# The second tile's q taken by the casting queue, the start of an attention-plus-feed-forward kernel put in a new order, and the first tile's denominators by halves

## Chip, cores, metric

One core of one Trainium2 chip. The metric is the time of one execution on the device in microseconds (us), inputs and outputs in device memory. The runs of one kernel in one block lie within 0.3 us (after_again) to 3.7 us (q_early) of each other, so small differences are judged over several runs on the same chip. On one core a run counts as fast unless it is over 1.5% above the fastest of its kernel; all runs told here are within that (the two single looks have no state of their own).

## The reference, cut to what matters

```python
# attention without softmax: 8 batches, 8 heads, 576 positions, head size 64
r_q, r_k = maximum(q, 0), maximum(k, 0)
q_p = concat(r_q * cos_w, r_q * sin_w)      # cos_w, sin_w depend on the position
k_p = concat(r_k * cos_w, r_k * sin_w)
kv  = einsum('bhsf,bhsd->bhfd', k_p, v)
den = einsum('bhsf,bhf->bhs', q_p, sum(k_p, axis=2)) + 1e-6
x   = einsum('bhsf,bhfd->bhsd', q_p, kv) / den
# feed-forward: x is [4608, 512], inner size 1536
g   = x @ w_gate
out = (g * sigmoid(g) * (x @ w_val)) @ w_out
```

All of it is float32 outside; the kernel multiplies in bf16.

## The kernel before, the parts that matter

The 576 positions of a batch lie in nine slots of 64. A tile is two slots, 128 rows of x. For the first four tiles the order of work at the start is a hand-laid list of words that a loop turns into instructions.

```python
CUT = (4, 7)
first = {"q": consts.tile([P, G, CUT[0], D], FP32, name="first_q")}
...
def load_first(nm, gs, lo=0, hi=NC):          # SyncE's queue, float32
    nc.sync.dma_start(out=first[nm][:, gs, lo:hi]..., in_=source(0, nm)[:, gs, lo * D:hi * D])
KCUT = 5
load_first("v", slice(0, 2))
load_first("v", slice(2, 4))
load_first("q", slice(0, G), 0, 2)            # slots 0, 1: tile 0
load_first("k", slice(0, 2))
load_first("k", slice(2, 4), 0, KCUT)
load_first("k", slice(2, 4), KCUT, NC)
load_first("q", slice(0, G), 2, 4)            # slots 2, 3: tile 1, last in this queue
...
def load_slots(b, nm, lo, hi):                # GpSimd's queue: casts to bf16 on the way
    nc.gpsimd.dma_start(out=raw_of(b, nm)[:, :, lo:hi]..., in_=source(b, nm)[:, :, lo * D:hi * D])
...
nc.gpsimd.tensor_copy(out=hold, in_=first["v"][:, 1, 0, 0:1])   # GpSimd waits for the first half of v
load_slots(0, "q", CUT[0], NW)                # slots 4 to 7
load_w(0, 1); load_w(1, 1); ...               # then the weights, k and v of batch 1, and so on
...
words = """
    cq0@act cq1@act tq0 qr0@dve rk1.0@act rk0.0@dve qw0.0 qw0.1 z6 kv0.0 rk2.0@act rk3.0@dve rk2.1@act
    kv1.0 kvo01@dve rk3.1@act cq3@dve kv1.1 cq2@dve kvo00@dve tq1 kvo10@act a0.0 qr1@dve kvo11@act qw1.1
    z2 a0.1 qw1.0 tq2 den0 rec0 a1.0 x0.0 qr2@act tq3 x0.1 xt0.0 a1.1 qw2.0 xc0.0@act xt0.1 qw2.1
    ... """
```

The words: cq casts q of one slot to bf16; tq transposes a tile's q on TensorE; qr is its relu; qw weights it with cos and sin; rk is the relu of a piece of k; kv the products k times v; kvo copies them out of PSUM; a are the products of a tile's q with kv; den, rec, x make x from them; xt and xc turn x; G, s, V, m are the feed-forward part; z are idle products on zeros that keep TensorE busy. After the @ stands the engine (act is ScalarE, dve VectorE).

## Time and profile before

| | before |
|---|---|
| time, median of 3 runs | 327.97 us (327.35 to 328.61) |
| span of the profiled run | 326.1 us |
| TensorE busy | 318.7 us, 98% |
| TensorE idle, waiting for q of tile 1 | 1.71 us |

TensorE is busy nearly all the time, so busy shares say little. What can be won is read from the list of its waits and from its timeline before 20 us. Both are in the prediction.

### The profile page before, as it was taken

What the parts mean: (1) busy time and instruction counts of PE and PEld (TensorE: products, weight loads), DVE (VectorE), ACT (ScalarE), POOL (GpSimd) and SP (SyncE); (2) the same over time, 40 slices, a digit from 0 to 9 for tenths busy, and PEclk for the clock granted to TensorE, in tenths of its full rate; (3) what the DMA queues carried; (4) which work ended last, traced back from release to release, by engine and by line L of the source; (5) the groups of instructions that cost most, each with busy time, mean ns of one, the idle gap of its engine ahead of it and who ended that gap; (6) DMA issues with size and microseconds to landing.
All of it is one profiled execution on the core that took longest, in us unless ns stands there. A gap on an engine that the chain in (4) does not pass through costs nothing.

```text
span 326.1 us, 6192 instructions
## 1 busy us (share of the span) xinstructions
PE 318.7 (98%) x2459; PEld 165.0 (51%) x2470; DVE 182.3 (56%) x367; ACT 132.8 (41%) x248; POOL 34.1 (10%) x57
## 2 busy tenths in 40 slices
PE   8799999999999999999999999999999999999995
PEld 4488855454545444544454445444454445444443
DVE  7594857885575655575557555655664145423420
ACT  7353456843463336423543344343432133213311
POOL 6654300002001100020002000200000000000000
PEclk9999999999999999999999999999999999999999
DMA  7999999398867997799598949795921411140014
GB/s 259 224 199 197 207 204 211 62 132 137 162 117 95 163 140 146 110 157 158 121 124 127 181 110 136 108 184 116 138 51 34 99 32 32 36 105 21 2 32 97
DMA packets 71660, 40.51 MB, mean 124 GB/s; under 512 B 46672, under 2 KB 66384, under 8 KB 71632
## 3 DMA queue, kind: packets, MB, share of 16 engines
q1 hardware_dynamic: 49808, 22.55, 39.0%
q0 software_dynamic: 21664, 17.44, 35.2%
q8 instruction: 19, 0.31, 0.4%
q10 hardware_dynamic: 160, 0.13, 0.1%
q14 instruction: 9, 0.07, 0.1%
HBM read 37.75 MB, written 9.44 MB: 145 GB/s over the span
## 4 chain that ended last, share of the span: by engine, by line
PE 94%; DMA 3%; SPq 1%; issue 0%; ACT 0%; DVE 0%; ACTq 0%; DVEq 0%
PE banks L503 57%; PE banks L539 28%; DMA first_q<-in_q_dram 3%; PE banks L276 3%; PE banks L390 2%; SPq L116 1%; PE banks L475 1%; PE banks L434 1%; PE banks L372 1%; PE banks L558 1%; PE banks L264 0%; PE banks L149 0%; ACT ob L561 0%; PE banks L351 0%; DVE qf L339 0%
## 5 line engine op out<-in xcount | busy, mean ns | idle before, releaser
L514 DVE TENSOR_TENSOR ht<-sg,banks 128x512 bf16<-128x512 bf16 (+2 forms) x122 | 76.0, 625 | 67.2 <-PE banks L503 60.9
L509 ACT ACTIVATE sg<-banks 128x512 bf16<-128x512 f32 (+2 forms) x122 | 66.9, 548 | 113.8 <-PE banks L503 108.7
L503 PE MATMUL banks<-xT,wv_sb 128*128 128x512 bf16 (+2 forms) x488 | 112.8, 355 | 0.0
L503 PE MATMUL banks<-xT,wg_sb 128*128 128x512 bf16 (+2 forms) x488 | 112.8, 355 | 0.0
L539 PE MATMUL banks<-wo_sb,ht 128*128 128x512 bf16 x409 | 93.5, 379 | 0.6
L503 PEld LDWEIGHTS <-wv_sb 128*128 128x128 bf16 x488 | 47.1, 98 | 46.4
L503 PEld LDWEIGHTS <-wg_sb 128*128 128x128 bf16 x488 | 45.7, 98 | 41.5
L539 PEld LDWEIGHTS <-ht 128*128 128x128 bf16 x420 | 40.0, 98 | 45.2 <-issue 0.4
L546 ACT COPY ob<-banks 128x512 f32<-128x512 f32 x18 | 10.6, 586 | 51.4 <-PE banks L539 49.4
L232 DVE TENSOR_TENSOR r_q<-raw_q,tab 128x1152 bf16<-128x1152 bf16 x24 | 17.9, 753 | 20.2 <-ACT raw_q L215 20.2
L546 DVE COPY ob<-banks 128x512 f32<-128x512 f32 x17 | 11.7, 691 | 28.9 <-PE banks L539 28.0
L236 DVE TENSOR_TENSOR v<-raw_v,tab 128x1152 bf16<-128x1152 bf16 x31 | 23.0, 751 | 0.3 <-ACT raw_v L570 0.3
L411 DVE TENSOR_TENSOR x<-banks,rec 128x512 bf16<-128x512 f32 (+1 forms) x32 | 21.5, 674 | 1.1
L714 POOL COPY hold<-phit 1x2 bf16<-1x2 bf16 x5 | 0.9, 176 | 156.6 <-DMA phit<-r_q 156.6
L215 ACT ACTIVATE raw_k<-raw_k 128x576 bf16<-128x576 bf16 x24 | 16.0, 675 | 0.0
L215 ACT ACTIVATE raw_q<-raw_q 128x576 bf16<-128x576 bf16 x24 | 15.7, 680 | 0.5 <-DMA raw_q<-in_q_dram 0.5
L390 PEld LDWEIGHTS <-phit 128*128 128x128 bf16 (+1 forms) x240 | 9.9, 100 | 6.0 <-issue 1.3
L390 PE MATMUL banks<-kv,phit 128*128 128x65 bf16 (+1 forms) x240 | 11.5, 195 | 0.0
L149 PE MATMUL banks<-zeros 128*128 128x64 bf16 (+1 forms) x66 | 9.9, 310 | 1.0 <-DVE zeros L144 1.0
L299 DVE CAST kv<-banks 64x260 bf16<-64x260 f32 x12 | 5.1, 428 | 7.5 <-ACT kv L299 7.4
L276 PEld LDWEIGHTS <-raw_k 64*64 64x64 bf16 x504 | 7.5, 106 | 2.6 <-issue 2.1
L276 PE MATMUL banks<-v,raw_k 64*64 64x130 bf16 x504 | 8.7, 218 | 0.0
(80 smaller groups left out, 136.3 us busy)
## 6 DMA issues: line engine op xcount, KB each, us to landing
out_dram<-ob SPq DMA_DIRECT2D x70, 128.0 KB, 2.4
raw_k<-in_k_dram POOLq DMA_DIRECT2D x7, 576.0 KB, 9.7
raw_q<-in_q_dram POOLq DMA_DIRECT2D x6, 576.0 KB, 6.1
raw_v<-in_v_dram POOLq DMA_DIRECT2D x6, 576.0 KB, 12.3
wo_sb<-in_moe_w_out_dram POOLq DMA_DIRECT2D x3, 512.0 KB, 12.3
wg_sb<-in_moe_w_gate_dram POOLq DMA_DIRECT2D x5, 256.0 KB, 10.6
wv_sb<-in_moe_w_val_dram POOLq DMA_DIRECT2D x5, 256.0 KB, 10.0
wo_sb<-in_v_dram SPq DMA_DIRECT2D x2, 576.0 KB, 4.1
```

What stands on the lines that cost most here:

```text
L149: nc.tensor.matmul(out=ps, lhsT=zeros, rhs=zeros[:, 0:cols].unsqueeze(1).to_broadcast([P, 4, cols]), start=True, stop=True)
L215: nc.scalar.activation(out=out, in_=in_, func=AF.Relu)
L232: nc.vector.tensor_tensor(out=st[b, "q"][:, g], in0=o.unsqueeze(2).to_broadcast([P, NC, 2, D]), in1=tab, op=ALU.mult)
L236: nc.vector.tensor_tensor(out=v2s[b % 2][:, g, :, :, 0:D], in0=(first if b == 0 and g == 0 else {"v": raw_of(b, "v")})["v"][:, g].unsqueez ...
L276: nc.tensor.matmul(out=ps[i * D:(i + 1) * D, e, j * 2 * D1:(j + 1) * 2 * D1], lhsT=raws[b, "k"][es, g, c], rhs=v2s[b % 2][es, g, c, :, 0:D ...
L390: nc.tensor.matmul(out=ps[ms, e, g * D1:(g + 1) * D1], lhsT=phit[b][:, e, g, c:c + n].rearrange("p c s -> p (c s)"), rhs=kv2s[b % 2][:, e, ...
L411: nc.vector.tensor_tensor(out=st["x", t].rearrange("p (y e d) -> p e y d", e=2, d=D)[:, :, ys], in0=ps[:, :, 0:2 * J * D1].rearrange("p e ...
L503: nc.tensor.matmul(out=st["f", tg, fc, lo][i], lhsT=(wg_sb, wv_sb)[i][:, kc, fs], rhs=xT[tg][:, ts, kc], start=(kc == 0), stop=(kc == KC - 1))
L509: nc.scalar.activation(out=sg[:, 0:n], in_=st["f", tg, fc, lo][0], func=AF.Silu)
L514: nc.vector.tensor_tensor(out=hts[tg % 2][:, fc, r:r + n], in0=st.pop(("s", tg, fc, lo))[:, 0:n], in1=ps[1], op=ALU.mult)
L539: nc.tensor.matmul(out=o_ps[t], lhsT=hts[tg % 2][:, fc, r:r + P], rhs=wo_sb[:, fc], start=(fc == 0), stop=(fc == FC - 1))
L546: (nc.scalar.copy if t % 2 == 0 else nc.vector.tensor_copy)(out=ob, in_=ps)
```

## The change

Three intents. The q of tile 1 no longer waits at the end of SyncE's queue to be cast by VectorE: it comes first on GpSimd's queue, in bf16. The order of the first four tiles is computed anew. And the denominators of tile 0 are added and inverted for half of the heads at a time, so that the first half of its x is ready before the second half of its products. The pools of x and sg get one buffer more, and the two halves of tile 4's products, later on, come directly behind each other. The diff, its core (cut: line shifts, small renamings, the rest of the words; the comments are mine):

```diff
-    xp = ctx.enter_context(tc.tile_pool(name="xp", bufs=3))
+    xp = ctx.enter_context(tc.tile_pool(name="xp", bufs=4))
-    sgp = ctx.enter_context(tc.tile_pool(name="sgp", bufs=4))
+    sgp = ctx.enter_context(tc.tile_pool(name="sgp", bufs=5))
-    first = {"q": consts.tile([P, G, CUT[0], D], FP32, name="first_q")}
+    first = {"q": consts.tile([P, G, QCUT, D], FP32, name="first_q")}      # QCUT = 2
-    load_first("q", slice(0, G), 2, 4)
-                if t < 2:
+                if t == 0:             # tile 1 is transposed from raw_q too
-    load_slots(0, "q", CUT[0], NW)
+    load_slots(0, "q", QCUT, 4)
+    load_slots(0, "q", 4, NW)
-    def x_den(t, ps):
+    def x_den(t, ps, ys=slice(0, 4)):  # x_rec likewise: by halves of the heads
     words = """
-        cq0@act cq1@act tq0 qr0@dve rk1.0@act rk0.0@dve qw0.0 qw0.1 z6 kv0.0 rk2.0@act rk3.0@dve rk2.1@act
-        kv1.0 kvo01@dve rk3.1@act cq3@dve kv1.1 cq2@dve kvo00@dve tq1 kvo10@act a0.0 qr1@dve kvo11@act qw1.1
-        z2 a0.1 qw1.0 tq2 den0 rec0 a1.0 x0.0 qr2@act tq3 x0.1 xt0.0 a1.1 qw2.0 xc0.0@act xt0.1 qw2.1
+        cq1@act cq0@dve tq0 qr0@dve rk0.0@act rk1.0@dve qw0.0 qw0.1 z6 kv0.0 rk2.0@dve rk3.0@dve kv1.0
+        kvo01@act rk3.1@dve kvo00@act rk2.1@dve kv1.1 a0.0 kvo11@act kvo10@dve tq1 den0.0 rec0.0 a0.1 x0.0
+        qr1@act tq2 den0.1 rec0.1 qw1.1 tq3 qr2@act qw1.0 xt0.0 x0.1 a1.0 qr3@act a1.1 qw2.0 xt0.1 qw2.1
     ...
-    at((0, 0), lambda: kv_free(1), a_(4, 0))
-    at((0, 1), a_(4, 1))
+    at((0, 0), lambda: kv_free(1), a_(4, 0), a_(4, 1))
```

More of the change, by code (lines that the diff above doesn't have):

```diff
@@ L103, in load_slots @@
                             in_=source(b, nm)[:, :, lo * D:hi * D])
-    CUT = (4, 7)
+    QCUT = 2
+    CUT = 7
     wo_sb = consts.tile([P, FC, d_model], BF16)
     hts = [consts.tile([P, FC, T], BF16, name=f"ht_{i}") for i in range(2)]
-    first = {"q": consts.tile([P, G, CUT[0], D], FP32, name="first_q")}
+    first = {"q": consts.tile([P, G, QCUT, D], FP32, name="first_q")}
     for nm, home in (("v", wo_sb), ("k", hts[1])):
@@ L395, in a_tile2, with x_rec @@
         x_of(t, ps)
-    def x_den(t, ps):
-        den = smp.tile([P, H, 1], FP32, name="den")
+    def x_den(t, ps, ys=slice(0, 4)):
+        if ys.start == 0:
+            st["den", t] = smp.tile([P, H, 1], FP32, name="den")
         nc.vector.tensor_single_scalar(
-            out=den.rearrange("p (e y) o -> p e y o", e=2),
-            in_=ps[:, :, 0:2 * J * D1].rearrange("p e (y x) -> p e y x", x=D1)[:, :, :, D:D1], scalar=1e-6, op=ALU.add)
-        st["den", t] = den
-    def x_rec(t):
-        rec = smp.tile([P, H, 1], FP32, name="rec")
-        nc.vector.reciprocal(out=rec, in_=st.pop(("den", t)))
-        st["rec", t] = rec
-        st["x", t] = xp.tile([P, d_model], BF16, name="x")
+            out=st["den", t].rearrange("p (e y) o -> p e y o", e=2)[:, :, ys],
+            in_=ps[:, :, 0:2 * J * D1].rearrange("p e (y x) -> p e y x", x=D1)[:, :, ys, D:D1], scalar=1e-6, op=ALU.add)
+    def x_rec(t, ps, ys=slice(0, 4)):
+        if ys.start == 0:
+            st["rec", t] = smp.tile([P, H, 1], FP32, name="rec")
+            st["x", t] = xp.tile([P, d_model], BF16, name="x")
+        nc.vector.reciprocal(out=st["rec", t].rearrange("p (e y) o -> p e y o", e=2)[:, :, ys],
+                             in_=st["den", t].rearrange("p (e y) o -> p e y o", e=2)[:, :, ys])
     def x_mul(t, ps, ys=slice(0, 4)):
@@ L418, in x_of @@
         x_den(t, ps)
-        x_rec(t)
+        x_rec(t, ps)
         x_mul(t, ps)
@@ L584 @@
     load(1, "v", 2)
-    load_slots(1, "q", 0, CUT[1])
+    load_slots(1, "q", 0, CUT)
     load_wo(0)
@@ L588 @@
     load_wo(2)
-    load_slots(1, "q", CUT[1], NC)
+    load_slots(1, "q", CUT, NC)
     for nm in ("q", "k", "v"):
@@ L610, in q_ @@
     def q_(b, j, part, eng="act"):
-        lo, hi = ((0, CUT[b]), (CUT[b], NC))[part]
+        lo, hi = ((0, CUT), (CUT, NC))[part]
         return lambda: qturn_pe(b, j, lo, hi, eng)
     words = """
-        cq0@act cq1@act tq0 qr0@dve rk1.0@act rk0.0@dve qw0.0 qw0.1 z6 kv0.0 rk2.0@act rk3.0@dve rk2.1@act
-        kv1.0 kvo01@dve rk3.1@act cq3@dve kv1.1 cq2@dve kvo00@dve tq1 kvo10@act a0.0 qr1@dve kvo11@act qw1.1
-        z2 a0.1 qw1.0 tq2 den0 rec0 a1.0 x0.0 qr2@act tq3 x0.1 xt0.0 a1.1 qw2.0 xc0.0@act xt0.1 qw2.1
-        xc0.1@act den1 z2 a2.0 rec1 qr3@act G1.0 x1.0 a2.1 G0.0 s1.0 V0.0 qw3.0 s0.0 xt1.0 qw3.1 V1.0
-        xc1.0@dve a3.0 a3.1 m0.0 G1.1 den3 G2.01 m1.0 s1.1 rec3 V1.1 x3.0 s2.01 G0.1 V0.1 s0.1 V2.01 m1.1
-        m0.1 xt3.0 den2 m2.01 G3.01 rec2 V3.01 x2.0 s3.01 G4.01 xc3.0@dve G5.01 s4.01 m3.01 xt2.0 s5.01
-        V4.01 xc2.0@dve V5.01 m4.01 G2.23 m5.01 G0.23 s2.23 V0.23 s0.23 G3.23 m0.23 V2.23 s3.23 G4.23 m2.23
-        V4.23 s4.23 V3.23 m4.23 G1.23 m3.23 V1.23 s1.23 G5.23 m1.23 V5.23 s5.23 m5.23
+        cq1@act cq0@dve tq0 qr0@dve rk0.0@act rk1.0@dve qw0.0 qw0.1 z6 kv0.0 rk2.0@dve rk3.0@dve kv1.0
+        kvo01@act rk3.1@dve kvo00@act rk2.1@dve kv1.1 a0.0 kvo11@act kvo10@dve tq1 den0.0 rec0.0 a0.1 x0.0
+        qr1@act tq2 den0.1 rec0.1 qw1.1 tq3 qr2@act qw1.0 xt0.0 x0.1 a1.0 qr3@act a1.1 qw2.0 xt0.1 qw2.1
+        xc0.0@act den1 z2 a2.0 rec1 xc0.1@act a2.1 x1.0 G1.0 G0.0 qw3.1 s1.0 xt1.0 s0.0 qw3.0 V0.0 xc1.0@act
+        V1.0 den2 rec2 a3.0 x2.0 a3.1 G0.1 G1.1 den3 s0.1 V1.1 rec3 s1.1 xt2.0 x3.0 G2.01 xc2.0@act V0.1
+        m1.0 V2.01 s2.01 m0.0 m0.1 xt3.0 m1.1 G3.01 m2.01 xc3.0@act V3.01 s3.01 G1.23 m3.01 V1.23 s1.23
+        G0.23 m1.23 V0.23 s0.23 G5.23 m0.23 G4.01 s5.23 G2.23 s4.01 G4.23 s2.23 G5.01 s4.23 V5.01 s5.01
+        V5.23 m5.01 G3.23 m5.23 V3.23 s3.23 V4.23 m3.23 V2.23 m4.23 V4.01 m2.23 m4.01
     """.split()
@@ L633 @@
         whole, a, part = b not in ("0", "1") or a != "0", int(a), int(b or 0)
+        ys = slice(0, 4) if whole else slice(2 * part, 2 * part + 2)
         if op == "z":
@@ L652 @@
         elif op == "den":
-            x_den(a, st["a", a])
+            x_den(a, st["a", a], ys)
         elif op == "rec":
-            x_rec(a)
+            x_rec(a, st["a", a], ys)
         elif op == "x":
-            x_mul(a, st["a", a], slice(0, 4) if whole else slice(2 * part, 2 * part + 2))
+            x_mul(a, st["a", a], ys)
             st["a", a, "n"] = st.get(("a", a, "n"), 0) + 1
```

## The prediction

> **What bounds the kernel now.** I read the page first: the engines' busy shares and the chain that ended last.
>
> ```profile
> PE 318.7 (98%) x2459; PEld 165.0 (51%) x2470; DVE 182.3 (56%) x367; ACT 132.8 (41%) x248; POOL 34.1 (10%) x57
> PE 94%; DMA 3%; SPq 1%; issue 0%; ACT 0%; DVE 0%; ACTq 0%; DVEq 0%
> PE banks L503 57%; PE banks L539 28%; DMA first_q<-in_q_dram 3%; PE banks L276 3%; PE banks L390 2%; SPq L116 1%; PE banks L475 1%; PE banks L434 1%; PE banks L372 1%; PE banks L558 1%; PE banks L264 0%; PE banks L149 0%; ACT ob L561 0%; PE banks L351 0%; DVE qf L339 0%
> ```
>
> TensorE is busy 98% of the span and is 94% of the chain. The only other thing of size on it is a transfer, first_q, 3%. Nothing in this change touches the matrix products of the feed-forward part (L503, L539), so the gain can only come from the few microseconds in which TensorE is not working. The list of waits of TensorE has all of them:
>
> ```profile
> PE banks L347 <- DVE qf L339: 1.7, 1, 1.7
> PE banks L149 <- DVE zeros L144: 1.0, 1, 1.0
> PE banks L316 <- ACT raw_k L215: 0.3, 1, 0.3
> ```
>
> One wait of 1.7 us matters; the 1.0 us is the start. The timeline shows where it stands:
>
> ```profile
> 11.96 0.73 PE L316 MATMUL banks<-v,raw_k 64*64 64x130 bf16 x16 [0.31 <-ACT raw_k L215]
> 13.76 0.58 DVE L339 CAST qf<-first_q 128x256 bf16<-128x256 f32 x2 [2.37 <-DMA first_q<-in_q_dram]
> 14.40 0.40 PE L347 MATMUL banks<-ident,qf 128*128 128x128 bf16 x4 [1.71 <-DVE qf L339]
> 14.97 0.59 PE L149 MATMUL banks<-zeros 128*128 128x512 bf16 x2
> 17.36 0.59 PE L149 MATMUL banks<-zeros 128*128 128x512 bf16 x2
> 17.79 0.45 PE L372 MATMUL banks<-kvd,qwT 128*128 128x130 bf16 x4
> 18.07 0.39 PE L503 MATMUL banks<-xT,wg_sb 128*128 128x128 bf16 x4
> ```
>
> The columns are start, duration, engine, line; the bracket is the idle time before and who ended it. The first k-v products end at 12.69. Then TensorE stands until 14.40, because the q of the second tile (slots 2 and 3) lands at 13.67 and VectorE casts it. From 14.40 on there is no idle time, but two pairs of idle products (L149) stand in for work that is not ready; the busy figure hides those. From 17.79 all is real work. The busy time by stretch says the same:
>
> ```profile
> 12.69:14.40 1.71, 0.00 (x1) 0.00 (x0) 0.64 (x3) 0.65 (x2) 0.74 (x1) 1.00 1.80 180
> 14.40:18.07 3.67, 3.64 (x49) 2.51 (x49) 3.38 (x12) 1.46 (x4) 3.03 (x5) 1.00 1.51 195
> 18.07:24.24 6.17, 6.17 (x85) 5.67 (x83) 5.47 (x18) 2.83 (x9) 3.60 (x5) 1.00 1.41 199
> 24.24:41.15 16.91, 16.91 (x158) 14.72 (x158) 11.22 (x26) 7.04 (x20) 6.69 (x9) 1.00 1.34 202
> ```
>
> After the length come TensorE, its weight loads, VectorE, ScalarE, GpSimd. From 14.40 to 18.07 VectorE is at 3.38 of 3.67 us: there it, not TensorE, sets the pace. From 18.07 TensorE does.
>
> [...] SyncE's loads arrive as float32 and need a cast (L339), GpSimd's raw_q is bf16 at once. [...] The q of slots 2 and 3 was issued last on SyncE's queue, behind all of k, and took longest:
>
> ```profile
> ht<-in_k_dram SPq DMA_DIRECT2D x1, 256.0 KB, 8.1
> first_q<-in_q_dram SPq DMA_DIRECT2D x1, 256.0 KB, 9.8
> raw_q<-in_q_dram POOLq DMA_DIRECT2D x1, 256.0 KB, 8.5
> wo_sb<-in_moe_w_out_dram POOLq DMA_DIRECT2D x1, 512.0 KB, 14.1
> ```
>
> (the last figure is us from issue to landing.) [...] in the listing of the changed kernel's instructions x of the first half now waits for TensorE. [...] the granted clock is 1.00 in all four stretches above, so no clock is to be won or lost.
>
> **The change part by part.**
> 1. *q of slots 2, 3.* Removed: one 256 KB load on SyncE's queue and two VectorE casts (0.58). Added: a casting load of the same source bytes, first on GpSimd's queue at 4.50, and eight half transposes (0.34 of TensorE, as the second and third tile's each took in the chain) for four whole ones (0.22 as for x): +0.12. When does it land? Slots 4 to 7, twice the source bytes, were first on that queue and landed 8.5 us after 4.50, at 13.0. The new load must share with k (last piece at 3.33 + 8.1 = 11.4), so I estimate 11 to 12. Slots 4 to 7 now come second, but SyncE's last load is gone; the same bytes stand before them, estimate 13.2 to 13.5.
> 2. *The head.* One cast of the first q goes to VectorE, which is free at 8.16; +0.3 us on the first transposes, absorbed because k lands only at 9.4. k's relu pieces go mostly to VectorE: after the weighting at 10.79, 0.31 + 0.31 for the first pieces, then the last (landed 11.4) 0.28 + 0.28, done at 12.0 where ScalarE was done at 12.22. The k-v products should end near 12.5 against 12.69.
> 3. *The first tiles, VectorE's chain.* From 12.53: copy of kv 0.43, den 0.16; then half of the products of tile 0 by TensorE[...] to 13.5; x first half 0.37; den and rec 0.4; weighting of tile 1, 0.68; x second half 0.34; weighting of tile 2, 0.68 (start to start in the rows L324, L399, L406, L411, L360 of VectorE's timeline, where one overlaps the next a little). Sum: 15.97. Before, that point was 17.75. The 1.8 us come from: kv's copy 1.74 us earlier (12.53 against 14.27), the relu of tile 1 (0.42) gone to ScalarE, less some 0.4 for the extra den and rec.
> 4. *TensorE.* Tile 2's products start at 16.0 instead of 17.79, and the second half of them (0.22) is now ahead of the first feed-forward product, which starts at 16.4. Against 18.07 that is 1.65, and with the 0.22 done early 1.85. Then x of tile 1 (den, rec, x: about 1.05 after 15.95) is ready at 17.05, while TensorE has two groups of 0.22 to do: a hole near 0.25. After that I find none by the same walk: tile 3's weighting ends at 17.75 as TensorE comes to it, the three copies of xT (0.42 each) have left VectorE for ScalarE.
> 5. *Later.* One more buffer for x and sg removes waits that cost nothing now. The products of tile 4 directly behind each other instead of apart: the same 0.37 and 0.34 of work, no gain.
>
> Net: 1.85 - 0.25 = 1.6 us, from 327.97 to 326.4. Cross-check by TensorE alone: hole removed 1.71, one of the two pairs of idle products removed 0.43, kv 0.2 sooner, longer transposes 0.12, new holes 0.6 (0.35 waiting for VectorE before 16.0, 0.25 after): 1.62.
>
> **The rivals.**
> *VectorE takes the place of the transfer.* If VectorE's chain runs slower (each wait between engines costs some 0.05 that I did not always count), the gain shrinks. For: 3.38 of 3.67 us busy[...]. Against: 1.7 us of its work (one relu, three copies of xT) was moved to ScalarE, which is idle for most of that time. This would leave 0.8 to 1.2: 326.8 to 327.2.
> *The casting queue is late.* If slots 2 and 3 land past 13, or slots 4 to 7 past 14.2, the hole comes back in part. For: in the first 12 us that queue got little. Against: at half the bytes and first in line it has over a microsecond of room. Result 327 to 328.
> *The weights become the bound.* GpSimd's queue is one unbroken stream up to 56 us, so its landings hardly move. The last part of wo lands at 31.8 + 14.1 = 45.9; the first use of it is at 48.15 in the chain (third piece of the first output tile): 2.2 us of room. A gain of 1.6 fits, more than 2.2 could not come through. wv's columns for the third product of the feed-forward land at 9.05 + 10.0 = 19.1 and are wanted near 19.7: tight. This caps the result at about 325.7.
> *Nothing moves.* If the new order stalls on banks between 17 and 22 us, where each group waits for ScalarE or VectorE to give one back, the gain is used up there: 328.
>
> **Range and chances.** The middle is the walk, 326.4. Low end: no new hole, 325.6, near the cap. High end: the casting queue or VectorE eats two thirds, 327.5; the three runs of before spread 1.26 us by themselves. 2% is 6.5 us, more than all idle time of TensorE together (7.4 with the start, of which 1.71 is in reach), so faster by 2% is out: 0.01. Slower by 2% would need a new stall of 6.5 us, 0.01. Within 2%: 0.98.
>
> **What would show it.** In the profile after: no idle before the first tile's products, at about 12.5; the casting load of slots 2 and 3 landing before 12.7; first L503 product at 16.4, a hole of some 0.2 to 0.3 before the transposes of x of tile 1; the k-v products of batch 1 (L276) at 40.4 instead of 42.05 and everything after shifted by the same amount; one wait of TensorE of at most 0.5 in the list in place of 1.7. I am wrong if TensorE waits for raw_q, or if the first L503 product comes later than 17, or if an early lead is lost again before 57 us to wo, wv or a bank.

## The result

The changed kernel took 326.31 us (median of 4, 326.06 to 326.73), the kernel before 328.29 (median of 4, 327.35 to 328.61). Ratios are the mean time of one kernel's fast runs over that of the other's of the same rounds, so not quite the ratio of the medians: 0.9946, 95% interval 0.992 to 0.9971. By the 2% rule that is the same; it is a gain of 1.8 us, clear of the noise, and inside the predicted range.

The chain that ended last, of the changed kernel (by engine):

```profile
PE 95%; DMA 2%; DVE 1%; ACT 0%; ACTq 0%; SPq 0%; issue 0%
```

The load of first_q is no longer in it. TensorE's waits (who for whom, us in total, times, longest):

```profile
PE banks L347 <- DVE qf L339: 1.7, 1, 1.7
PE banks L149 <- DVE zeros L144: 1.0, 1, 1.0
PE banks L372 <- DVE qwT L360: 0.6, 1, 0.6
```

A 1.7 stands in the first line again, but it is another wait: the transposes of tile 0, not of tile 1. The timeline of TensorE (start, duration, engine, line; in the bracket the idle time before) shows where:

```profile
8.88 0.40 PE L347 MATMUL banks<-ident,qf 128*128 128x128 bf16 x4 [1.68 <-DVE qf L339]
...
12.54 0.40 PE L372 MATMUL banks<-kvd,qwT 128*128 128x130 bf16 x4
12.87 0.41 PE L351 MATMUL banks<-ident,raw_q 128*64 128x128 bf16 x8
...
15.07 0.63 PE L372 MATMUL banks<-kvd,qwT 128*128 128x130 bf16 x8 [0.64 <-DVE qwT L360]
...
16.55 0.61 PE L504 MATMUL banks<-xT,wg_sb 128*128 128x128 bf16 x8
17.11 0.40 PE L476 MATMUL banks<-ident,x 128*128 128x128 bf16 x4
```

Only idle products stood before 8.88 in both kernels (their last ends earlier here), so of that 1.68 only the later start counts: 8.88 against 8.08. By the end of the k-v products it is made good (12.6 against 12.69). From there tile 0's products run at once, tile 1's transposes follow at 12.87 instead of 14.40, and the first feed-forward product (L504, L503 before) is at 16.55 instead of 18.07. The new casting loads land well ahead (issued at 4.69 and near 5.5; the last figure is us from issue to landing):

```profile
raw_q<-in_q_dram POOLq DMA_DIRECT2D x1, 128.0 KB, 6.3
raw_q<-in_q_dram POOLq DMA_DIRECT2D x1, 256.0 KB, 6.8
```

The k-v products of batch 1 start at 40.40 against 42.05, and the span is 324.3 against 326.1: a lead of 1.65 at 40 us, 1.8 at the end. So far it looks as the prediction's walk had it. The experiments ask which part of the change earned it.

### The profile page after: what moved, and what is told of

The parts are those of the page before. It is cut to its first block, busy times and chain, and to the rows that moved or that the text cites. A ratio compares the mean times of both kernels' runs of the same rounds, so it can differ in the third digit from the quotient of the medians.

```text
span 324.3 us, 6204 instructions
## 1 busy us (share of the span) xinstructions
PE 317.2 (98%) x2472; PEld 164.6 (51%) x2472; DVE 181.3 (56%) x366; ACT 133.5 (41%) x249; POOL 34.8 (11%) x58
## 4 chain that ended last, share of the span: by engine, by line
PE 95%; DMA 2%; DVE 1%; ACT 0%; ACTq 0%; SPq 0%; issue 0%
PE banks L504 58%; PE banks L540 28%; PE banks L276 3%; PE banks L390 2%; DMA wo_sb<-in_v_dram 2%; PE banks L435 1%; PE banks L476 1%; PE banks L372 1%; PE banks L149 1%; PE banks L559 1%; PE banks L264 0%; PE banks L316 0%; DVE v L236 0%; ACT ob L562 0%; ACT raw_v L571 0%; DVE qwT L360 0%
## 5 line engine op out<-in xcount | busy, mean ns | idle before, releaser
L504 PE MATMUL banks<-xT,wv_sb 128*128 128x512 bf16 (+2 forms) x488 | 112.3, 355 | 0.0
L504 PE MATMUL banks<-xT,wg_sb 128*128 128x512 bf16 (+2 forms) x488 | 112.3, 355 | 0.0
L504 PEld LDWEIGHTS <-wv_sb 128*128 128x128 bf16 x488 | 47.2, 98 | 46.4
L504 PEld LDWEIGHTS <-wg_sb 128*128 128x128 bf16 x488 | 45.7, 98 | 41.5
L547 ACT COPY ob<-banks 128x512 f32<-128x512 f32 x18 | 10.5, 585 | 50.7 <-PE banks L540 48.7
L149 PE MATMUL banks<-zeros 128*128 128x64 bf16 (+1 forms) x64 | 8.3, 288 | 1.0 <-DVE zeros L144 1.0
```

Source lines behind the costliest of these rows:

```text
L149: nc.tensor.matmul(out=ps, lhsT=zeros, rhs=zeros[:, 0:cols].unsqueeze(1).to_broadcast([P, 4, cols]), start=True, stop=True)
L504: nc.tensor.matmul(out=st["f", tg, fc, lo][i], lhsT=(wg_sb, wv_sb)[i][:, kc, fs], rhs=xT[tg][:, ts, kc], start=(kc == 0), stop=(kc == KC - 1))
L547: (nc.scalar.copy if t % 2 == 0 else nc.vector.tensor_copy)(out=ob, in_=ps)
```

## The experiments

Every run was correct. All with five rounds, except the two looks at the kernel before (one profile and one time each). Runs of one block shared a chip and the runs of the kernel before.

| run | what it is | median us (runs) | before, same rounds | ratio, 95% interval |
|---|---|---|---|---|
| after_again | the changed kernel | 325.93 (6) | 328.5 (27) | 0.9929, 0.991 to 0.9948 |
| q_only | only the q load changed | 325.80 (6) | the same | 0.9924, 0.9906 to 0.9942 |
| q_back | all but the q load | 327.75 (22) | the same | 0.9987, 0.9973 to 1.0001 |
| den_whole | changed, denominators whole | 325.94 (6) | the same | 0.9930, 0.9913 to 0.9947 |
| a4_back | changed, tile 4 apart | 325.89 (6) | 328.67 (11) | 0.9927, 0.9912 to 0.9942 |
| q_a4 | q load and tile 4 only | 325.86 (6) | the same | 0.9927, 0.9913 to 0.9941 |
| cq_rk_act | changed, ScalarE helps in the head | 325.82 (6) | the same | 0.9922, 0.9906 to 0.9937 |
| before_look | before | 327.05 (1) | | |
| k_hold | cq_rk_act, casting queue held back | 327.38 (22) | 327.76 (35) | 0.9982, 0.9969 to 0.9994 |
| q_early | before, q ahead of k's last piece | 328.58 (14) | the same | 1.0007, 0.9985 to 1.0029 |
| before_look2 | before | 328.38 (1) | | |
| z_fill | before, the hole filled | 327.52 (22) | 328.05 (27) | 0.9979, 0.9969 to 0.999 |

### The parts of the change, one at a time

**The changed kernel again (after_again).** No edit.

> The changed kernel unaltered, as the yardstick of this chip, and to see which parts of its head repeat. Theory: 1.6 to 2.0 us faster than the kernel before. In its first trace the second half of v landed at 6.46 (5.87 before) and the first transposes of q began at 8.88 (8.08 before). If that is the change (fewer bytes on one queue, more on the other), it repeats within 0.2 us; if it is chance, the second half of v lands anywhere from 5.8 to 6.5 and the first transposes move with it.

The gain was 2.3 us here (0.9929 of 328.3), more than the 1.8 of the first four runs and more than the 1.6 to 2.0 expected; the reason comes below. The second half of v landed at 1.27 + 5.0 = 6.3 and the first transposes began at 8.68. In the five profiles with VectorE casting q in the head they began at 8.45 to 8.88, in the three profiles of the kernel before at 7.62 to 8.23, so the later start is the change's. The landing of v is not: in den_whole and a4_back, with the same loads, it landed at 5.8 to 6.0, as before the change.

**Only the load (q_only).** The kernel before with (cut: QCUT = 2 and the smaller first_q):

```diff
-    load_first("q", slice(0, G), 2, 4)
-    load_slots(0, "q", CUT[0], NW)
+    load_slots(0, "q", QCUT, 4)
+    load_slots(0, "q", 4, NW)
-                if t < 2:
+                if t == 0:
-    ... rk3.1@act cq3@dve kv1.1 cq2@dve kvo00@dve tq1 ...
+    ... rk3.1@act kv1.1 kvo00@dve tq1 ...
```

> The kernel before with only the q of slots 2 and 3 taken by the casting queue (its load on the other queue and its two casts gone), old order, whole denominators, old pools. Theory that the wait for this q was the cost and the order adds to it: the wait of 1.7 us goes, the first tile's products start near 13, but VectorE's old chain (copy of kv, relu and weighting of tile 1, den, rec, x) stands, so 0.9 to 1.3 us faster than before. Rival that the order is what counts: under 0.5 us. Rival that the transfer is all: 1.6 us or more, the same as the whole change.

Measured: 325.80, as fast as the whole change (325.93). The expectation of 0.9 to 1.3 us was a miss; the rival that the load is all was right. With the old order TensorE has no wait left but that of the start, and its timeline reaches the feed-forward part no later than with the new one:

```profile
12.27 0.41 PE L351 MATMUL banks<-ident,raw_q 128*64 128x128 bf16 x8
12.61 0.41 PE L372 MATMUL banks<-kvd,qwT 128*128 128x130 bf16 x4
...
15.67 0.45 PE L372 MATMUL banks<-kvd,qwT 128*128 128x130 bf16 x4
15.96 0.38 PE L503 MATMUL banks<-xT,wg_sb 128*128 128x128 bf16 x4
```

The first feed-forward product is at 15.96 here and at 16.17 and 16.55 in the two profiles of the changed kernel. (In the old order it stands ahead of 0.22 us of tile 2's products, in the new order behind them; with that set right it is 16.18, within what the new order shows.) What the load gains is probably the earlier landing and not the saved cast: with its landing at 11.0 instead of 13.67 in the changed kernel, even the two casts (0.58 us), begun when VectorE's relus of k end at 12.12, would be done by 12.70, ahead of the transposes at 12.87. That is an estimate; a plain load on a third queue, with the casts kept, was not tried.

**All but the load (q_back).** The changed kernel with the q of slots 2 and 3 on SyncE's queue again, behind k, and `cq3@dve cq2@dve` just ahead of `tq1`; for want of space it lands in hts[0], unused until later.

> The changed kernel with only the q of slots 2 and 3 put back on the plain queue, behind k, with its two casts on VectorE just ahead of the transposes (it lands in the room of the first hidden tile, which is not written until about 19.7, because the space is used up); new order, split denominators and pools stay. Theory: TensorE again waits for VectorE's cast, 1.3 to 1.7 us between the first half of tile 0's products and the transposes of tile 1; time within 0.5 us of the kernel before. Rival that the order alone gives the gain: within 0.4 us of the changed kernel.

Measured: 327.75, the ratio to the kernel before 0.9987 with 1 inside the interval. TensorE waits for the cast again:

```profile
14.00 0.40 PE L349 MATMUL banks<-ident,qf 128*128 128x128 bf16 x4 [1.45 <-DVE qf L341]
```

So the load alone is enough for the whole gain, and without it most of the gain is lost. The rest of the change is not worth nothing here, though, as I first read it. The runs of both kernels mix two clocks (the end of the experiments says how they are told apart). Full-clock runs alone are 327.13 us (mean of 11) against 327.70 for the kernel before (12): 0.57 us less. So the rest gains some 0.6 us as long as q is late, and nothing once q is early (325.92 with it, 325.79 without). Which part of it does so was not tried.

**Whole denominators (den_whole).** The changed kernel with:

```diff
-    tq1 den0.0 rec0.0 a0.1 x0.0 qr1@act tq2 den0.1 rec0.1 qw1.1
+    tq1 a0.1 den0 rec0 x0.0 qr1@act tq2 qw1.1
```

> The changed kernel with the first tile's denominators and reciprocals taken whole (one add and one reciprocal after both halves of the products, in place of two of each with the products of the second half between them). Theory of the prediction, that the split costs some 0.4 us of VectorE and an alternation on the banks (0.3 us in which VectorE waits for TensorE): without it VectorE's chain is 0.1 to 0.4 us shorter and the kernel that much faster, or equal. Rival, the intent of the change: x of the first half is ready earlier with the split, so without it the kernel is 0.2 to 0.4 us slower.

Measured: 325.94 against 325.93. No difference, in either direction. VectorE's timeline says why. Split, in the changed kernel:

```profile
12.99 0.15 DVE L400 TENSOR_SCALAR den<-banks 128x4 f32<-128x4 f32 x1
13.18 0.18 DVE L408 RECIPROCAL rec<-den 128x4 f32<-128x4 f32 x1
13.66 0.42 DVE L412 TENSOR_TENSOR x<-banks,rec 128x256 bf16<-128x256 f32 x1 [0.30 <-PE banks L372]
...
15.93 0.15 DVE L400 TENSOR_SCALAR den<-banks 128x8 f32<-128x8 f32 x1
```

Whole, in this run:

```profile
13.54 0.17 DVE L400 TENSOR_SCALAR den<-banks 128x8 f32<-128x8 f32 x1 [0.58 <-PE banks L372]
...
15.99 0.16 DVE L400 TENSOR_SCALAR den<-banks 128x8 f32<-128x8 f32 x1
```

The first half's den does start earlier (12.99 against 13.54), but its x then stands 0.30 for TensorE's second half, and a second den and rec follow. At the next tile's den both are at the same point, 15.93 and 15.99. The wait of 0.30 is the one that the listing of the instructions announced: VectorE's x of the first half stands until TensorE's products of the second half, which the program puts in the same banks, are done (they run from 13.22 to 13.63, x starts at 13.66). What forces this wait was not shown.

**Tile 4 apart (a4_back).** The changed kernel with the last two lines of the diff undone.

> The changed kernel with the two halves of tile 4's products put apart again, a piece of the output product between them. In the traces with them together the stretch from the products of batch 1 (L276) to the first product of the second token group takes 15.01 us, with them apart 15.24. Theory [...]: 0.1 to 0.3 us slower than the changed kernel. Rival, the prediction's 'no gain': within 0.1 us.

Measured: 325.89 against 325.93 for the changed kernel in the block before, ratios 0.9927 and 0.9929. The rival, no gain, holds; the 0.23 us that I read from two traces was no effect on the time.

**The load and tile 4 (q_a4).** q_only with those two lines added.

> The kernel before with two parts of the change only: q of slots 2 and 3 by the casting queue, and tile 4's halves together. Old order of the beginning, whole denominators, old pools. Theory that these two are all that gains and that the new order of the beginning costs as much as it brings: 0.1 to 0.3 us faster than q of slots 2 and 3 alone (ratio 0.9924 to the kernel before), so about 325.6, and at least as fast as the changed kernel. Rival, that the new order gains something that the first call did not show: 0.2 us or more slower than the changed kernel.

Measured: 325.86. Not faster than q_only; as fast as the changed kernel, from which it leaves out the new order, the split and the buffers.

Two builds went to no chip. With sg at four buffers the new order comes to a deadlock in the build, so that fifth buffer is needed by the order. With x at three buffers it builds.

### What the floor is

**ScalarE helps in the head (cq_rk_act).** The changed kernel with `cq0@act cq1@act tq0` and `rk2.0@act rk3.0@dve rk2.1@act` in place of `cq1@act cq0@dve tq0` and four rk pieces on VectorE (rk3.1 stays there; the words around it change places a little).

> The changed kernel with VectorE relieved ahead of the k-v products: both casts of the first q on ScalarE, as before, and two of the four relu pieces of k's second half on ScalarE, which stood idle for 2.05 us there. Theory that VectorE bounds the head of the new order (it casts q only after v, and does five relu pieces one after another): first transposes near 8.4 instead of 8.7 to 8.9, k-v products done 0.2 to 0.5 us earlier, the kernel 0.2 to 0.4 us faster than the changed one. Rival, that the landing of k's last piece (near 11.0) or of q bounds it: under 0.1 us.

Measured: 325.82, against 325.89 for a4_back in the same block: inside the noise, so the theory of a gain falls. The first transposes did begin earlier, at 8.32, but then VectorE waits for the last piece of k:

```profile
11.22 0.29 DVE L217 TENSOR_SCALAR raw_k<-ht 128x256 bf16<-128x256 f32 x1 [0.29 <-DMA ht<-in_k_dram]
```

**The casting queue held back (k_hold).** cq_rk_act, and GpSimd waits for the first q instead of v:

```diff
-    nc.gpsimd.tensor_copy(out=hold, in_=first["v"][:, 1, 0, 0:1])
+    nc.gpsimd.tensor_copy(out=hold, in_=first["q"][:, 1, 0, 0:1])
```

> The changed kernel with ScalarE's share of the head (as in the last call) and one more edit: GpSimd's first casting load waits for the first q (lands near 7.5) in place of the first half of v (near 4.5), so 3 us of GpSimd's traffic no longer run beside k. All versions with q on the casting queue end at 325.8 to 325.9 whatever their order; their k-v products start their last part when k's last piece lands, 10.6 to 11.5. Theory that this landing is the floor, and that the two queues share the transfer engines: k's last piece lands 0.3 to 0.8 us earlier, the k-v products end as much earlier, and the kernel is 0.2 to 0.6 us faster, unless q of slots 4 to 7 now lands after 13.2 and takes it back. Rival, the order or VectorE is the floor: no change within 0.1 us though k lands earlier.

Measured: 327.38, 1.5 us slower than the changed kernel had been on another chip; by the ratios to the kernel before, 0.9982 against 0.9922 for cq_rk_act, some 2 us. k's last piece did land earlier, at 3.33 + 6.5 = 9.8 instead of 11.2 (10.6 and 11.1 in the two profiles of the changed kernel), and tile 0's products started at 11.27 instead of 12.23, both against cq_rk_act. So the two queues do take time from each other: 0.8 to 1.4 us of k's landing here. (The packets of both are counted on the same 16 transfer engines; in the kernel before, from 9.7 to 10 us, those of SyncE's queue took 59.1% of the engines' time and those of the casting queue 72.5%, some at once.) But the loads on the casting queue came later: q of slots 4 to 7 at about 13.7, the proviso of the expectation. TensorE's waits:

```profile
PE banks L351 <- DMA raw_q<-in_q_dram: 1.5, 1, 1.5
PE banks L149 <- DVE zeros L144: 1.0, 1, 1.0
PE banks L264 <- DMA raw_q<-in_q_dram: 0.6, 1, 0.6
PE banks L276 <- DVE v L236: 0.4, 1, 0.4
PE banks L540 <- DMA wo_sb<-in_moe_w_out_dram: 0.2, 1, 0.2
```

1.5 us for q of slots 4 to 7, then three more waits further on, for q and v of batch 1 and for wo: 2.7 us in all beyond the start. This is near the third rival of the prediction: with some 3 us of delay the stream on the casting queue becomes the bound. Whether the versions at 325.8 are all held by k's landing is not shown, since this run moved both edges at once.

**The same load earlier in the same queue (q_early).** The kernel before with its last two load_first lines exchanged.

> The kernel before with one edit: on SyncE's queue the q of slots 2 and 3 is issued ahead of k's last piece, not after it. Nothing else moves. Theory that the bytes ahead of a load decide, not the queue as such: this q lands near 11.5 to 12, k's last piece 0.7 to 2.5 us later than before (12 to 14), and the wait moves from q to the k-v products; gain between 0 and 1 us, less than by the casting queue. Rival, that q's place at the end of this queue was all: as fast as by the casting queue (ratio 0.993).

Measured: 328.58, ratio 1.0007: no gain, at the low end of the expectation (full-clock runs alone: 327.47, mean of 7, against 327.41, of 22). The rival falls. q was cast at 11.62, some 1.3 to 2.1 us sooner than in the profiles of before, but now k's last piece is late:

```profile
13.55 0.73 PE L316 MATMUL banks<-v,raw_k 64*64 64x130 bf16 x16 [2.26 <-ACT raw_k L215]
```

The hole is the same kind in another place. Ahead of k's last piece or behind it on SyncE's queue, one of the two pays. With q on the casting queue TensorE waits for neither: its list of waits for the changed kernel has no raw_k and no raw_q. Putting q ahead of all of k was not tried.

### Why the gain was 2.3 us and not 1.8

The kernel before does not have one time. In the first block its 27 runs fall in two groups, 327.38 to 328.02 and 328.44 to 329.20, and so do those of q_back; the three versions of this block with q on the casting queue lie within 325.4 to 326.3.

**Two looks at the kernel before (before_look, before_look2).** No edit.

> The kernel before once more, one profile. Its 27 runs of the first call fall in two groups, 327.4 to 328.0 and 328.4 to 329.2, and so do those of the version with q put back on the plain queue; no version with q on the casting queue shows it. The first profile was in the lower group. If this one falls in the upper group, theory: the q of slots 2 and 3 (or something ahead of it on its queue) lands 0.8 to 1.3 us later than at 13.67, and TensorE's wait for it is that much longer. Rival: the wait is the same and the time is lost elsewhere, then the two groups have nothing to do with this load.

The first look was in the lower group: 327.05. Its cast of q started at 12.97, 0.79 sooner than in the first profile, and its time was 0.87 less. That suggested that q's landing sets everything.

> The kernel before once more, one profile. So far: 327.92 us with the cast of q of slots 2 and 3 starting at 13.76, and 327.05 us with it starting at 12.97: 0.87 us against 0.79. Theory that the landing of this load sets the time of the kernel before one to one: here the time is 327.05 plus the difference of this start to 12.97, within 0.2 us. Rival: other causes move it by more than that.

The second look fell in the upper group, 328.38, with its cast at 12.95, like the first look. By my theory it should have been 327.03. The theory failed by 1.35 us. The clock is the difference. Busy time by stretch of 1 us, first for before_look (start and end; length, then TensorE, weight loads, VectorE, ScalarE, GpSimd, granted clock, transfers, GB/s):

```profile
15.00:16.00 1.00, 0.98 (x20) 0.57 (x16) 0.93 (x5) 0.60 (x1) 0.99 (x2) 1.00 1.55 193
```

and for before_look2:

```profile
14.00:15.00 1.00, 1.00 (x13) 0.71 (x10) 0.80 (x4) 0.00 (x0) 1.00 (x2) 0.90 1.63 173
15.00:16.00 1.00, 1.00 (x14) 0.63 (x13) 0.93 (x5) 0.10 (x1) 0.96 (x2) 0.50 1.53 194
17.00:18.00 1.00, 1.00 (x9) 0.89 (x9) 0.49 (x3) 0.40 (x2) 0.61 (x2) 0.50 1.45 195
18.00:19.00 1.00, 1.00 (x13) 0.72 (x12) 0.97 (x3) 0.85 (x2) 0.40 (x2) 0.89 1.45 196
```

From about 14.8 to 18.2 (worked out from the 0.90 and 0.89 of the stretches at either end) TensorE ran at half clock. Its busy figure does not tell: 0.98 at full clock in before_look, 1.00 at half clock here. The work between the transposes of tile 1 and the first feed-forward product took 4.90 us (13.74 to 18.64), where before_look needed 3.67 (13.52 to 17.19): 1.23 us lost. The hole before it was longer:

```profile
13.74 0.40 PE L347 MATMUL banks<-ident,qf 128*128 128x128 bf16 x4 [2.02 <-DVE qf L339]
```

2.02 us here, 1.72 and 1.71 in the two profiles at full clock. The profile of q_early, with its hole of 2.26, also shows 0.50 to 0.52 from 15 to 18 us.

**The hole filled (z_fill).** The kernel before with five idle products in the hole:

```diff
-    ... kv1.1 cq2@dve kvo00@dve tq1 ...
+    ... kv1.1 z5 cq2@dve kvo00@dve tq1 ...
```

> The kernel before with one edit: five idle products (512 columns, some 1.1 us) between the last k-v products and the transposes that wait for q of slots 2 and 3. Everything else as before, the late q too. The second look at the kernel before (328.38 us) had its q at the same time as the first look (327.05 us), but from 14.9 to 18.1 us its granted clock was 0.50; the hole of 2.02 us came just before. Theory that the upper group of times of the kernel before is this half clock, called by the hole: with the hole filled the upper group is gone, no run above 328.1, the spread of runs under 1.3 us where the kernel before spreads over 2, the mean 0.4 to 0.9 us below that of the kernel before in the same rounds, though the wait for q is still there; and still 0.9 us or more slower than q by the casting queue (325.8). Rival, that the half clock comes from elsewhere and the hole has no part in it: two groups as before, mean within 0.2 us of the kernel before.

Measured: 327.52, mean 327.51 against 328.15 for the kernel before in the same rounds, 0.64 us less, by an edit that adds work and leaves the late q as it was. Of 22 runs one is above 328.1 (328.37), of the 27 of the kernel before 13 are. Two small misses: I had said none, and a spread under 1.3 us, where it is 1.63. The profiled run waits as before for q, but for less, with the clock at 1.00 throughout:

```profile
12.72 1.25 PE L149 MATMUL banks<-zeros 128*128 128x512 bf16 x5
14.41 0.40 PE L347 MATMUL banks<-ident,qf 128*128 128x128 bf16 x4 [0.44 <-DVE qf L339]
```

The record holds one thing more that I had overlooked: each run's mean granted clock. It parts the two groups without a miss. In the first block the 15 runs of the kernel before from 328.44 us up have a mean clock of 0.992 to 0.995, the 12 others 0.997 to 1.000. (3.4 us at half clock in a span of 326 lower the mean to 0.995.) In the block of z_fill 13 of its 27 runs are low, 0.992 to 0.995; of the 22 runs of z_fill none is below 0.998. So the one run above 328.1 is not the half clock come back, and the mean of z_fill, 327.51, is close to that of the full-clock runs of the kernel before, 327.64: what filling the hole gains is the half clock and little else.

Within the first block the gain can now be parted. Full-clock runs alone: 327.70 for the kernel before (mean of 12), 325.92 for the changed kernel (6), 325.79 for q_only (6), a gain of 1.8 and 1.9 us for the late q itself. The low runs are 1.15 us slower than the full-clock ones (328.85), which makes 0.64 us of the mean. In q_back 11 of 22 runs are low, in q_early 7 of 14, in k_hold 3 of 22; in the versions with q on the casting queue and not held back, none.

## Why the prediction was right, and where not

- *The bound and the time.* Predicted 326.4 and a gain of 1.6; measured 326.31 and 1.8 in the first comparison, 1.8 between the two profiled spans, both at full clock. Right. The landmarks of the walk held closely in that profile: tile 1's den at 15.93 (15.97 said), tile 2's products at 16.08 (16.0), the first feed-forward product at 16.55 (16.4), the k-v products of batch 1 at 40.40 (40.4). That they agree to 0.1 us is partly luck: in the second profile of the same kernel the first three stand at 15.56, 15.71 and 16.17, some 0.4 earlier.
- *The casting load.* Said to land at 11 to 12, with slots 4 to 7 at 13.2 to 13.5; landed at 11.0 and near 12.3, the latter a microsecond sooner than said. The rival of a late casting queue did not occur; k_hold shows what it would have cost.
- *The new order and the split.* The step that failed is the attribution. I read the 1.8 us of VectorE's chain as the work of the new order (relu moved to ScalarE, less the cost of the split). Point 15.95 was right, but the old order with the new load is as fast (q_only), and the split changes nothing (den_whole: 15.99 against 15.93). What ended was the wait; both orders then fit. Walking only the changed kernel, and not the load alone, hid this.
- *The holes.* Said: 0.35 for VectorE and 0.25 before the transposes of x of tile 1. Measured: 0.64 for VectorE and hardly any before those transposes (0.02 of issue time, and the transposes 0.35 in place of 0.22). The sum was said to be 0.6 and came out near it, at 0.66 and another 0.13 in the transposes, by errors that partly cancel. The cross-check also has +0.12 for longer transposes of tile 1, which falls away: in the chain that it was read from, the four whole ones that go took 0.40 (L347) and the eight halves 0.34 (L351).
- *The head.* I had 0.3 us for the cast behind v on VectorE; it was 0.8 in the first profile. It was absorbed, as said: the k-v products ended at 12.6 all the same, since k's last piece landed earlier too (3.33 + 7.3 = 10.6 against 11.4). That was luck: the two looks at the kernel before also have it at 10.5 and 10.6.
- *The list of waits.* "At most 0.5 in place of 1.7" was wrong: 0.6, and a 1.7 at the start that costs little.
- *The clock.* "No clock is to be won or lost" was wrong. In the one profile I had, the clock was 1.00; about half of the runs of the kernel before (15 of 27, 13 of 27) have a mean clock of 0.992 to 0.995, 1.15 us each in the first block and some 0.6 us of the mean. In before_look2, the one such run of that kernel with a profile, the half clock came after the hole.
- *Buffers.* "Removes waits that cost nothing now" was wrong for sg: the new order does not build without the fifth. Tile 4's halves: no gain, as said.

## What to carry to other kernels

When a change bundles one moved load with a new order of everything around it, try the load alone: here the load was the whole gain, and the new order, the split and the buffers could have been left out. A load that stands last on a queue can come too late by its place alone: here its cast began at 12.95 to 13.76 from the last place and at 11.62 from the place before it. Putting it one place earlier only made the next load late (q_early, a hole of 2.26 us), another queue served both (325.80 us, q_only), and delaying that other queue cost more than it gave (k_hold: k's last piece 0.8 to 1.4 us sooner, then 2.7 us of other waits). And a short hole in TensorE can cost more than its length: here holes of 2.02 and 2.26 us, which ended at 13.74 and 13.55, were followed by a granted clock of 0.50 from about 14.8 and 15 us on, and the low-clock runs of the kernel before were 1.15 us slower; after holes of 1.71 and 1.72 us the profiles show 1.00. Why it comes in some runs only was not shown. Look at the granted clock in the microseconds after it, in more than one profile, at whether the runs fall in two groups, and at the mean clock recorded with each run.
